# A hand-written order of 1,087 operations replaced by a new one, with four of six groups of filler matmuls left out

## The chip, the core and the metric

The kernel runs on one core of a Trainium2 chip. The metric is the device time of one execution in microseconds (us); lower is better. The engines named below are PE (TensorE, the matmuls), DVE (VectorE), ACT (ScalarE), POOL (GpSimd) and SP (SyncE, which issues nearly all DMAs).

## What is computed

The reference is a block with two residual halves on an input of 2048 rows and 640 columns, all in bf16, with scales and shifts made from a vector `c`:

```python
mod = (silu(c) @ w_mod)                     # sa, ca, ga, sb, cb, gb: 640 each
h = layernorm(A_q) * (1 + ca) + sa
k_shift = short_conv(A_k, shift_k)          # four taps along the rows
kv = k_shift * A_v
y = irfft(rfft(kv, 4096) * rfft(ssm_k, 4096))[:2048] + kv * ssm_D
x = A_q + ga * (h * y)                      # first half: long convolution
h = layernorm(x) * (1 + cb) + sb
z = gelu(h @ w_in)                          # 2 x 864 columns
z2 = layernorm(z[:, 864:])
g = w_sp @ z2 + b_sp                        # the mix: 2048 x 2048 over the rows
out = x + gb * ((z[:, :864] * g) @ w_out)
```

## The kernel before

**Convolution.** The 640 columns are cut into five units of 128. For each unit the filter (K) and the signal (U) go through the same steps. `stage1` multiplies the data by a table and leaves the tile `X1`. `forward` (line 432) makes eight blocks of frequencies in the PSUM tile `pu`. For K, `k_item` copies a block into a tile `KH` on ACT. For U, `u_item` multiplies `pu` by `KH` on DVE (the product of line 463, in `Tf` or `T`). In half of the blocks two sums on POOL or DVE follow (line 477, tile `W`). PE then multiplies back into `pz` (`inv`), and ACT or DVE copies the result into `Z`. The signal itself comes from `short_conv`: PE applies the four taps, DVE multiplies by v (line 570), and two DMA transposes of unit 0, or one of each other unit, regroup the result (line 582, tile `X`). For units 0 to 3 a DMA transpose turns `Z` into the single buffer `ZT` (line 708). PE makes y from it and DVE multiplies y into `gh` (line 701). Unit 4 is turned on PE instead (line 744). k and v of units 1 and 2, and of units 3 and 4, lie together in one buffer each (`kv_home`, line 512); this is the same in both kernels.

**First normalization and modulation.** `xt` is read in four DMAs of 640 KB (line 589). `ln1` takes statistics of each of 16 row tiles, on DVE (lines 603 and 604) or ACT (599 and 600). `mod` loads a slice of `w_mod` (line 643) and multiplies by `silu(c)`.

**Second half.** For each of four groups of four row tiles, `z_group` normalizes x, turns it (group 0 on PE, line 881; the others by a DMA transpose, line 912) and applies scale and shift (`hmod`, line 894, and `hmod2`, line 920). It then does 16 products with `w_in` of five matmuls of 432 columns. Each goes to a buffer `pu` or `pz`, and there are two of each. ACT applies gelu (line 943) and so frees the buffer. DVE takes statistics of the second half (line 949). POOL makes the reciprocal deviation `rstdz` (line 190), DVE makes `nmrz` (line 958), and `zn` on DVE (966) or ACT (964) normalizes.

**The mix.** The product with `w_sp` uses seven block products instead of eight, on sums made by DVE (lines 1011 and 1021). The seven products of the first pair of row tiles (`prodw`) stand in the ordered list. Pairs 1 to 7, with the projection by `w_out` (line 1160), follow as plain code.

**What sets the order.** Every operation up to and with the first pair is entered in a list (`Plan.op`) with the engines that may run it and what it depends on. `Plan.run` then issues the operations in the order of the string `ORDER`, on the engine that its letter names (P, A, D, G for POOL, S for SP):

```python
for e, i in order:
    o = self.ops[i]
    assert e in o["eng"] and done.issuperset(o["deps"]), (e, i)
    o["fn"](engines[e])
    done.add(i)
```

Each engine runs its own operations strictly in that order. An operation whose input or buffer is not ready holds up all that stand behind it on its engine, DMAs on SP included. A filler is a group of matmuls of the identity whose result nobody reads. They have no effect on the output:

```python
for j in range(k):
    mm(p_[:, 0:2], ident[:], ident[:, None, :].to_broadcast([P, S1C, P]), j == 0, j == k - 1)
```

Before, six groups of 4, 6, 2, 2, 4 and 3 of them stand in the list, as operations 1033 to 1038.

Of the kernel before, what the change touches and what calls it, by code (L numbers as in the profile page):

```python
# [30 lines left out]
PE_FLIPS = (4,)  # L31
TB = 4
NQ = DU // 4
FILLS = (4, 6, 2, 2, 4, 3, )
MODE = ('susussus', 'susussus', 'susussus', 'susussus', 'susussus')
SLOTS = dict(Tf=2, W=2, X=4, X1=4, KH=7, T=2, Z=3, ZT=1, wm=1, big=2, dg=2, st1=2, s1=1, sm=2, pu=2, pz=2)
PSUM_TAGS = ("s1", "sm", "pu", "pz")


ORDER = """  # L40
D0 P1034 A1 P7 D18 D128 D13 D15 A4 S89 D14 A16 D101 S2 G5 D6 P8 G102 D103 D116 D117 A10 A11 P1038 A28 A129 S90 D91 D17
P1035 A118 A119 S23 P146 P149 D104 S25 D105 A106 A107 D27 P1036 A147 P29 A148 P31 G108 S24 A150 G109 S26 D92 P155 D110
D111 A112 D151 A113 A156 G120 G121 P152 A154 A153 G114 D30 D32 G115 D20 P33 D122 D123 A124 A157 A125 G126 S524 D34 P35
D36 S525 D528 D529 D530 P1033 P158 A159 P162 A163 P134 P164 A135 A165 P166 A167 P137 D19 A21 P140 D141 P168 G127 S93
A169 P170 S37 S38 A171 D138 P172 A173 D94 P228 A229 D22 P174 A176 G139 P177 A179 D531 D175 D178 P234 S39 D235 G136 G41
P180 A181 D182 D532 P183 P230 A184 G53 A185 P186 D187 G142 A231 P202 D203 G42 P43 A533 D130 P232 G188 D189 S40 D44 P45
D46 S52 P196 D197 A534 G198 G199 S527 P160 A161 P190 A191 A233 P49 D50 P47 G54 D48 P212 P204 P248 S3 A535 P200 A205 P9
A249 P143 D213 G214 G215 D543 A12 G67 G131 G132 P222 A144 G145 D223 P55 D56 P192 D193 D536 G537 P59 D60 A544 A545 S51
P57 P252 A253 D58 P206 D207 G208 G209 P194 A201 S566 P218 D219 D538 G550 G551 P254 A195 A255 S526 D539 D540 P567 A568
S95 P569 A570 P258 A259 P216 P236 A237 P242 A243 G224 G225 P256 D257 P238 A217 A239 A541 P61 D62 S571 D96 S65 P210 S64  # L50
G66 P240 A241 P260 P220 D261 A211 G554 A546 P302 A303 P292 G555 G556 G557 A221 P574 G262 G263 D542 G552 D293 D547 P246
A247 P226 A227 S63 P572 P286 D287 D288 D553 P304 A305 D573 P264 A265 P250 A251 G78 P294 A295 P308 A309 D575 D652 G548
D549 G562 D592 P296 D297 G289 P276 A558 G298 P68 P306 S576 D277 P72 D615 P244 P290 A133 D559 A307 P270 D271 P326 A245
D69 P278 A291 G563 G564 P316 D73 A327 A565 D598 A317 P266 P328 A329 A279 D267 G299 P300 D301 P577 P314 S97 A315 P330
A331 G272 G273 D594 P324 A325 G613 D650 D578 S77 D593 D614 P70 D71 A560 A561 G617 P310 A311 P332 A333 G595 D714 D671
P280 D281 P74 D98 P579 D596 D75 P322 A323 P274 P350 A79 D351 G282 P376 A377 G283 P344 D345 D580 G654 A275 P268 A269
P334 D335 P378 G599 A379 P80 D597 P312 S600 A313 D81 P284 G346 G347 P320 P601 D602 A285 A321 P380 G336 G337 D708 G709
P366 A381 P370 D367 D371 P82 P382 A383 P318 G619 A319 P603 P338 P348 A349 A339 D83 S76 P388 A389 P400 D604 P605 D606
A401 S99 D100 P360 D361 P352 A353 P386 A387 P402 D620 G618 G372 G373 A403 P607 D608 P374 D375 P398 A399 G362 P354 G363
D355 G610 D356 G357 D616 P404 G653 A405 P364 P86 P384 A365 G656 P406 A407 D87 A385 P340 D341 P84 P368 D85 P408 P414  # L60
D409 A369 P450 P342 A451 P390 S621 P622 D415 G710 A391 G711 G677 D623 G410 G411 P454 A455 P418 P396 D419 A343 P624
P358 S581 P452 A397 D625 A453 G651 G420 D421 P392 P440 A393 P626 D627 P412 D441 G657 P456 A359 P428 G678 A413 G655
A457 D429 G430 G431 P628 D629 G630 P416 A417 P394 A395 P422 D423 S88 P474 A475 P464 A465 D635 P444 D445 G446 P582 A583
P480 A481 D636 P424 D425 P442 A443 D675 G676 D637 P458 A459 G447 P476 A477 D638 P434 D435 P426 D427 P472 A473 S658
P659 D660 P478 A479 P432 P466 P661 A433 P482 P448 A467 D609 D632 A449 D662 P663 G436 G437 P438 A439 P462 A463 D483
P498 D664 P665 D499 G673 G484 G485 P518 P486 D519 P502 D503 D504 P500 A501 G674 P460 A461 P468 A469 D666 P488 D489
A487 S584 G672 P585 A586 P508 G520 G521 P522 G505 A523 G668 D509 P492 D493 P506 A507 P470 A471 S679 P680 D681 P514
D515 G510 P490 A491 G511 G494 G495 P512 G715 G667 D634 A513 P682 D683 P516 A517 D631 P684 D685 P496 S757 D639 D633
P686 D687 D688 D690 A497 P720 A721 P716 G693 P722 P718 D717 P724 D719 P726 A723 P727 D689 P725 D728 G698 D729 D730
D759 D731 D760 G761 D696 D732 D733 D692 D762 G763 D735 A764 S587 P588 A589 P736 P1037 P590 A591 D734 D691 D772 D773  # L70
G774 P750 P765 D737 D738 D767 D769 D768 P766 A771 A770 D775 P743 D741 D837 G712 D697 P792 D751 S758 A777 P815 A816
D694 G776 P779 A783 A784 D742 P785 D739 D835 A786 D695 D740 P778 D836 D838 D752 A793 D713 D744 D745 G703 G839 D840
G841 G842 D843 P788 D782 A789 D781 D780 G612 D794 P795 A796 P817 P819 D670 D797 D669 D702 D700 D706 D611 G640 D642
A844 S845 D749 A818 P799 A800 G847 D641 D644 A820 D747 D902 P821 G846 D705 D701 D801 D645 D699 A822 P823 A824 D643
D904 P802 A803 D804 P806 A807 P825 A826 D805 A848 P813 A850 P827 A828 P809 A810 D849 A814 P851 A852 D746 P875 A876
D901 P879 A880 P858 A859 D748 D903 D790 D787 D811 P872 A873 D808 G905 D906 P865 S1046 P889 A866 A890 D648 P881 D704
A882 D756 D646 D812 D753 D967 D907 D909 G908 D754 D1050 P861 A862 D1047 P854 A855 D867 P893 A894 S1042 P883 A884 D798
G910 S911 P887 A888 A916 P891 A892 D877 P868 A869 D647 D968 P885 A886 D755 D969 D649 D707 D970 D1051 G971 D972 S1040
D791 S1039 A973 D976 D914 D975 D974 D853 D1052 G912 S1045 G913 G915 D856 P959 A960 P917 A918 D857 G829 D830 S977 G982
D874 D878 P947 A948 D834 D831 D860 D832 D833 D1063 D870 P920 A921 P924 A925 P938 A939 S1044 D863 D864 P931 S1041 D1055  # L80
D1056 P941 A942 D1058 D926 D979 G980 P927 A928 A932 G978 D1048 P953 D919 D933 D871 D929 P934 D940 P949 A954 D922 A981
P1000 D1054 P997 D923 S1043 A935 D936 G895 D896 D899 D1059 A950 P983 D930 A998 D999 D1060 A1001 D1002 A984 D943 D944
A898 A900 P993 A994 P1007 A1008 D937 D1057 G961 D897 D1064 D962 P1004 D985 D963 P990 P986 A987 D988 D989 A991 D992
D995 D996 A1005 D1006 P951 D1003 A952 A964 D965 P1025 P1015 A1016 D1009 D1010 A1026 D966 D1067 G1027 D1028 P955 A956
P945 A946 P957 D1030 P1021 A1029 P1013 D1032 A1022 A1014 P1071 P1073 A958 D1031 D1068 P1082 D1065 D1066 P1078 D1069
D1070 A1072 P1075 D1079 A1074 D1083 P1077 D1076 D1080 P1084 P1011 A1012 D1085 P1017 A1018 P1019 A1020 S1081 D1062
S1086 D1049 P1023 A1024 D1053 D1061
"""


# [39 lines left out]
def kernel(  # L130
# [79 lines left out]
    with ExitStack() as pctx:  # L210
# [758 lines left out]
        for g in range(NT // TB):  # L969
            z_group(g)  # L970
        for i, k in enumerate(FILLS):
            def fill(e, i=i, k=k):
                p_ = new("fill%d" % i, "s1", [P, S1C, 2 * NJ * 4], F32)
                for j in range(k):
                    mm(p_[:, 0:2], ident[:], ident[:, None, :].to_broadcast([P, S1C, P]), j == 0, j == k - 1)
# [258 lines left out]
```

## Time and profile before

| | |
|---|---|
| time, median of 3 runs | 312.26 us (312.03 to 312.69) |
| the profiled execution, its own time | 312.08 us |
| its span, first to last instruction | 310.0 us |
| PE busy | 296.2 us, 96% |
| DVE busy | 259.6 us, 84% |
| ACT busy | 157.0 us, 51% |
| POOL busy | 123.0 us, 40% |
| DMA moved | 42.63 MB, mean 137 GB/s |

Times within the execution count from the start of the span. A row of the profile gives the source line, the engine, the operation as output <- input, and how often it occurs. After a bar, or in brackets, stands the idle time of the engine before it and what ended it. "Busy" of PE is modelled, since matmuls overlap; how far apart they start tells more. Convolution and modulation fill the first 132 us. The products with `w_in` and the first pair of the mix go on to 205 us, and pairs 1 to 7 fill the rest.

### The profile page before, as it was taken

Reading aid. Unit: us, or ns where it says so; the run is one execution under the profiler, and the core shown is the slowest. Engines: PE = TensorE matmul, PEld = TensorE weight load, DVE = VectorE, ACT = ScalarE, POOL = GpSimd, SP = SyncE. Lnnn points to the kernel's source line nnn. Section 1 sums busy time; section 2 is a strip of 40 time slices with the busy share of each in tenths; the row PEclk is TensorE's granted clock in tenths of the full one; section 3 lists DMA queues with packets and bytes.
Section 4 is the critical chain, followed back from the end, with each engine's and each line's share of the span. In section 5 each row is a group of like instructions: output and inputs, shape, how many; then the busy total and the mean of one; then the engine's idle time right before and its main releaser. Section 6 shows DMA issues by size and latency. Waiting matters only on the chain.

```text
span 310.0 us, 6894 instructions
## 1 busy us (share of the span) xinstructions
PE 296.2 (96%) x2746; PEld 207.1 (67%) x2746; DVE 259.6 (84%) x528; ACT 157.0 (51%) x282; POOL 123.0 (40%) x157
## 2 busy tenths in 40 slices
PE   6989999999999998999999997999999999999996
PEld 2779898889999887755554553555565656555564
DVE  7999899999899999999969998957676858567474
ACT  5899899897969755476665684040101010010100
POOL 2663788859899696676342522000000000000000
PEclk9999999999999999999999999999999999999999
DMA  7999989986396779204999900092939395640614
GB/s 147 275 176 250 244 220 252 225 169 132 26 231 134 173 134 323 76 3 85 216 175 147 183 2 2 0 140 63 194 89 187 63 176 111 129 102 0 104 30 114
DMA packets 122963, 42.63 MB, mean 137 GB/s; under 512 B 108751, under 2 KB 122932, under 8 KB 122932
## 3 DMA queue, kind: packets, MB, share of 16 engines
q1 hardware_dynamic: 122778, 42.16, 64.6%
q8 instruction: 21, 0.34, 0.4%
q14 instruction: 10, 0.08, 0.1%
q10 hardware_dynamic: 154, 0.05, 0.1%
HBM read 16.11 MB, written 2.62 MB: 60 GB/s over the span
## 4 chain that ended last, share of the span: by engine, by line
PE 63%; DVE 25%; DMA 4%; issue 3%; ACT 2%; POOL 2%; POOLq 1%; DVEq 0%; ACTq 0%
PE ps L1036 23%; PE pu L244 12%; PE po L1160 10%; PE pz L244 8%; PE sm L244 4%; DVE st L949 3%; DVE Tf L463 3%; DMA ZT<-Z 3%; PE s L244 2%; PE pz L1036 2%; DMA KH<-in_c_dram 2%; DVE T L463 2%; DVE X L570 2%; DVE gh L684 1%; DVE st L603 1%
## 5 line engine op out<-in xcount | busy, mean ns | idle before, releaser
L244 PEld LDWEIGHTS <-Z 128*128 128x128 bf16 x320 | 30.9, 98 | 28.2 <-POOL Z L920 1.5
L244 PE MATMUL pu<-X,M 128*128 128x128 bf16 (+1 forms) x480 | 45.7, 237 | 1.9 <-ACT X L247 0.7
L244 PEld LDWEIGHTS <-M 128*128 128x128 bf16 x480 | 37.3, 98 | 6.3 <-issue 3.1
L1036 PEld LDWEIGHTS <-S 128*128 128x128 bf16 x256 | 25.0, 98 | 24.0 <-issue 2.4
L1042 ACT COPY m<-ps 128x432 f32<-128x432 f32 x7 | 3.6, 519 | 72.7 <-PE ps L1036 72.7
L477 POOL TENSOR_TENSOR W<-Tf 128x256 bf16<-128x256 f32 x45 | 33.2, 759 | 10.2 <-DVE Tf L463 8.3
L247 ACT CAST X<-s 128x1024 bf16<-128x1024 f32 x30 | 30.6, 1021 | 4.9 <-PE s L244 4.5
L1160 PE MATMUL po<-w_o,uT 128*128 128x320 bf16 (+2 forms) x231 | 32.7, 295 | 0.0
L244 PE MATMUL pz<-big,Z 128*128 128x432 bf16 x160 | 32.4, 346 | 0.3 <-POOL Z L920 0.3
L244 PE MATMUL pu<-big,Z 128*128 128x432 bf16 x160 | 32.3, 346 | 0.3 <-DVE Z L894 0.3
L463 DVE TENSOR_TENSOR Tf<-pu,KH 128x1024 f32<-128x1024 f32 x25 | 30.2, 1216 | 2.0 <-PE pu L244 1.7
L1036 PEld LDWEIGHTS <-wT 128*128 128x128 bf16 x192 | 18.7, 98 | 15.2
L1160 PEld LDWEIGHTS <-uT 128*128 128x128 bf16 (+1 forms) x231 | 22.2, 98 | 9.7
L244 PEld LDWEIGHTS <-G 128*128 128x128 bf16 x330 | 24.8, 98 | 1.7 <-issue 0.2
L247 ACT CAST Z<-pz 128x512 bf16<-128x512 f32 x36 | 20.9, 596 | 7.7 <-PE pz L244 7.5
L247 ACT CAST KH<-pu 128x512 bf16<-128x512 f32 x40 | 23.4, 595 | 2.1 <-PE pu L244 1.8
L1036 PE MATMUL ps<-X,wT 128*128 128x432 bf16 x112 | 22.7, 346 | 0.0
L1036 PE MATMUL ps<-T,S 128*128 128x432 bf16 x112 | 22.7, 346 | 0.0
L1036 PE MATMUL ps<-X,S 128*128 128x432 bf16 x112 | 21.6, 346 | 0.0
L244 PEld LDWEIGHTS <-X 128*128 128x128 bf16 x288 | 17.9, 97 | 4.8 <-issue 1.6
L244 PE MATMUL sm<-dg,big 128*128 128x128 bf16 x320 | 20.5, 219 | 0.2 <-DVE gca_bf L671 0.2
L244 PEld LDWEIGHTS <-big 128*128 128x128 bf16 x320 | 18.8, 98 | 0.6 <-issue 0.3
(189 smaller groups left out, 563.5 us busy)
## 6 DMA issues: line engine op xcount, KB each, us to landing
wm<-in_w_mod_dram SPq DMA_DIRECT2D x6, 800.0 KB, 5.6
xt<-in_A_q_dram SPq DMA_DIRECT2D x4, 640.0 KB, 7.3
out_dram<-ot SPq DMA_DIRECT2D x15, 160.0 KB, 2.0
big<-in_B_w_in_dram SPq DMA_DIRECT2D x2, 1080.0 KB, 5.9
X<-in_A_ssm_k_dram SPq DMA_DIRECT2D x4, 512.0 KB, 7.0
big<-in_A_v_dram SPq DMA_DIRECT2D x2, 1024.0 KB, 6.3
w_o<-in_B_w_out_dram SPq DMA_DIRECT2D x6, 160.0 KB, 3.0
X<-in_A_ssm_k_dram SPq DMA_DIRECT2D x2, 256.0 KB, 3.8
```

The costliest lines, as they stand in the source:

```text
L244: nc.tensor.matmul(o, lhsT=w, rhs=x, start=start, stop=stop)
L247: (e.copy if e is nc.scalar else e.tensor_copy)(dst, src)
L463: e.tensor_tensor(T_[:], (tl[pu] if src is None else tl[src])[:, :, :, None, :].to_broadcast(shape), tl[KH][:, :, None, :, :].to_broadcast ...
L477: e.tensor_tensor(tl[W][:, :, o, :], T_[:, :, 0, o, :], T_[:, :, 1, 1 - o, :], op=ALU.add if o else ALU.subtract)
L570: e.tensor_tensor(tl[kv][:].rearrange("p c (n g) -> p n c g", g=8)[:, 4 * i:4 * i + 4], tl[ps][:].rearrange("p a (c g) -> p a c g", g=8), ...
L603: e.bn_stats(out=st[:, a, :], in_=xt[:, n, a * HS:(a + 1) * HS])
L684: lambda e, vec=vec, o=o: e.tensor_tensor(gvu, gvu, vec[:, None, d0:d0 + du].to_broadcast([P, TB, du]), op=o),
L949: op("D", "stz", lambda e, i=i, n=n, fc=fc: e.bn_stats(out=stz[:, n, fc, :], in_=tl[z2][:, i, fc * FC:(fc + 1) * FC]), r=[(z2, (i, fc))], ...
L1036: nc.tensor.matmul(ps[:, :FC], lhsT=lhs[:, s_, :], rhs=rhs(s_), start=(s_ == 0 and not more), stop=(s_ == HT - 1), skip_group_check=more)
L1042: nc.scalar.copy(part[p, m][:], part[p, BANK[m]][:, :FC])
L1160: nc.tensor.matmul(ps[:, :hi - lo], lhsT=uTs[t][:fsz[ft], ft, :], rhs=w_o[:fsz[ft], ft, lo:hi], start=(ft == 0), stop=(ft == NFT - 1))
```

## The change

Two things differ in the file: the tuple `FILLS` and the string `ORDER`. No function is changed. Operations up to 1032 keep their numbers; the later ones fall by four, because four fillers are gone (`prodw` 1071 is now 1067).

```diff
-FILLS = (4, 6, 2, 2, 4, 3, )
+FILLS = (4, 6)
...
-D0 P1034 A1 P7 D18 D128 D13 D15 A4 S89 D14 A16 D101 S2 G5 D6 P8 G102 D103 D116 D117 A10 A11 P1038 A28 A129 S90 D91 D17
-P1035 A118 A119 S23 P146 P149 D104 S25 D105 A106 A107 D27 P1036 A147 P29 A148 P31 G108 S24 A150 G109 S26 D92 P155 D110
...
-P945 A946 P957 D1030 P1021 A1029 P1013 D1032 A1022 A1014 P1071 P1073 A958 D1031 D1068 P1082 D1065 D1066 P1078 D1069
-D1070 A1072 P1075 D1079 A1074 D1083 P1077 D1076 D1080 P1084 P1011 A1012 D1085 P1017 A1018 P1019 A1020 S1081 D1062
-S1086 D1049 P1023 A1024 D1053 D1061
+A4 A1 S89 D101 G5 D0 D18 P1033 G102 D103 D110 P7 S2 D13 D6 S90 D19 A21 P8 D111 A11 A112 D14 A10 D20 D22 D15 S23 D27
+S26 P1034 A16 D17 D91 P146 A28 A113 G114 A147 D92 P152 D104 D105 A107 A106 D148 A154 A153 D116 D117 P155 D157 G108
...
+D992 D996 D1043 D1006 D1010 P1021 D962 D965 A963 P957 A960 A1016 P1013 A1022 D964 A958 D966 D1063 P1067 P1025 G1027 D1028
+A1029 A1014 A1032 A1026 P955 D1060 P1069 D1061 D1030 D1031 D1062 A1070 D1064 A956 D1065 D1066 A1068 S1038 P1074 D1075
+P1078 S1037 D1079 P1071 D1055 P1073 D1072 D1076 P1080 D1081 S1077 P1011 A1012 P1019 A1020 P1017 A1018 P1023 A1024
+D1057 S1082 D1049 D1044 D1056 D1058
```

Per engine, the new list makes these changes. Eleven filler matmuls are gone; ten remain, four at the start and six right after the small transposes. Some operations change engine:

| operation (line) | DVE | ACT | POOL |
|---|---|---|---|
| sums of a product (477) | 5 -> 11 | | 45 -> 39 |
| copy of the back-transform table (247, `G`) | 2 -> 4 | 2 -> 0 | |
| first normalization `xn` (629, 631, 633) | 2 -> 4 | 4 -> 4 | 10 -> 8 |
| `stage1` copies (247, `X`) | 6 -> 5 | 42 -> 43 | |
| copies into `Z` (247) | 4 -> 3 | 36 -> 37 | |
| copies of unit 4's turned `Z` (247, `X`) | 2 -> 1 | 2 -> 3 | |
| residual sum (721) | 12 -> 10 | | 9 -> 11 |
| normalization of z2, `zn` (964, 966) | 12 -> 9 | 4 -> 7 | |
| second normalization `zx` (866, 868, 870) | 6 -> 6 | 4 -> 5 | 6 -> 5 |
| `hmod2` (918, 920) | 3 -> 2 | 4 -> 5 | 8 -> 8 |

SP issues the same 59 operations of the list in another order. Up to the second quarter of `xt` and its neighbours:

```
before: ... v0 v0' xt0 xt1 ldX1 | regroup0 regroup0' | k1 v12 k2 xt3 c ...
after:  ... v0' v0 k0' ldX1 xt0 k1 | regroup0 regroup0' | xt1 v12 xt3 k2 c ...
```

The first half of `w_in` (1080 KB, line 846) stood after the fourth transpose of `Z` into `ZT`. It now stands between the regrouping of unit 4 and the third transpose of `Z`. In the second half the order of SP changes too:

```
before: turn1 w_out w_sp turn2 w_sp w_sp bias turn3 w_sp w_sp w_sp
after:  turn1 w_sp w_sp w_out turn2 w_sp turn3 bias w_sp w_sp w_sp
```

More of the change, by code (lines that the diff above doesn't have):

```diff
@@ L40 @@
 ORDER = """
-D0 P1034 A1 P7 D18 D128 D13 D15 A4 S89 D14 A16 D101 S2 G5 D6 P8 G102 D103 D116 D117 A10 A11 P1038 A28 A129 S90 D91 D17
-P1035 A118 A119 S23 P146 P149 D104 S25 D105 A106 A107 D27 P1036 A147 P29 A148 P31 G108 S24 A150 G109 S26 D92 P155 D110
-D111 A112 D151 A113 A156 G120 G121 P152 A154 A153 G114 D30 D32 G115 D20 P33 D122 D123 A124 A157 A125 G126 S524 D34 P35
-D36 S525 D528 D529 D530 P1033 P158 A159 P162 A163 P134 P164 A135 A165 P166 A167 P137 D19 A21 P140 D141 P168 G127 S93
-A169 P170 S37 S38 A171 D138 P172 A173 D94 P228 A229 D22 P174 A176 G139 P177 A179 D531 D175 D178 P234 S39 D235 G136 G41
@@ L46 @@
[L46 to L84, printed above, removed]
-P945 A946 P957 D1030 P1021 A1029 P1013 D1032 A1022 A1014 P1071 P1073 A958 D1031 D1068 P1082 D1065 D1066 P1078 D1069
@@ L86 @@
-D1070 A1072 P1075 D1079 A1074 D1083 P1077 D1076 D1080 P1084 P1011 A1012 D1085 P1017 A1018 P1019 A1020 S1081 D1062
-S1086 D1049 P1023 A1024 D1053 D1061
+A4 A1 S89 D101 G5 D0 D18 P1033 G102 D103 D110 P7 S2 D13 D6 S90 D19 A21 P8 D111 A11 A112 D14 A10 D20 D22 D15 S23 D27
+S26 P1034 A16 D17 D91 P146 A28 A113 G114 A147 D92 P152 D104 D105 A107 A106 D148 A154 A153 D116 D117 P155 D157 G108
+A156 A115 P29 S25 D30 P149 A150 A151 D122 G109 D123 A125 A119 S24 P33 D34 A124 A118 G120 G121 S93 D94 S524 D128 G126
@@ new lines @@
+P35 A129 G42 P162 D36 S39 G127 P31 D32 P228 S37 S38 D528 A163 A229 P158 A159 S525 P137 P164 A165 D529 D530 D138 P234
+P166 A235 S40 P168 P134 A167 D135 P230 A169 A231 G54 P172 A173 P174 D531 D175 G136 A176 P232 D53 D130 P140 S527 A233
+P180 D181 A182 P170 A171 P183 D185 A184 P177 P45 A179 A178 P186 D532 G139 A533 A534 A535 P202 D141 D187 D203 G41 P43
+D44 D46 G188 P196 P212 A543 G189 D197 P190 P204 G198 G199 A205 A191 D213 G214 G215 P47 D48 P49 D50 P160 A161 G142 D536
+G537 P192 D193 S52 P55 D56 P200 S3 P206 D207 G208 G209 P57 D58 A544 A545 P248 A249 P194 P143 D144 G145 P242 A201 S526
@@ new lines @@
+A195 D539 P218 D219 A243 P9 A12 G131 G132 D538 S51 P252 A253 G554 A546 P59 S566 D60 P222 P216 S95 D223 P254 A255 P236
+A237 A217 P567 A568 P569 P258 A259 S571 P246 A247 G555 P210 D540 D541 D542 P238 A239 G224 G225 D211 P226 P256 A257
+A570 P61 P240 A241 S65 D96 P302 D547 A227 G550 D62 P260 D261 D262 A303 P220 P286 D287 G556 P574 D575 G263 A221 P304
+A305 A67 G548 S64 P292 D293 G78 P264 P572 D573 G288 G289 D549 D558 S63 P250 A251 D66 P308 A309 S576 A562 A563 P296
+D297 P294 A551 P270 G559 G560 D271 G272 P306 P276 D277 A295 P70 P68 P266 D265 P244 A307 D267 D69 D71 A564 D565 D598
@@ new lines @@
+A245 P278 A279 P326 G561 P290 G654 D298 D299 A327 P316 A317 D596 P310 A311 G273 P274 S77 G552 D553 P328 A329 P314 P577
+P579 A315 P324 D675 D557 A325 D594 D578 D595 P330 A331 P322 A323 D708 D615 G616 D599 D580 A291 P72 S97 D73 P280 D281
+A275 G671 G282 G283 G655 S600 P332 A333 P74 P312 A313 P300 A301 D98 P376 G617 A377 D592 P344 D597 A79 P268 D75 A269
+D345 P350 D351 P378 A379 P284 G593 P334 D335 G336 D337 G346 P80 D81 P318 A319 S76 G619 P380 A381 P601 D602 P366 D367
+D347 G677 P320 G620 P338 A321 P382 A383 A285 P603 D604 P82 D83 P370 D371 G372 D373 A339 P388 A389 P348 P400 S99 A401
@@ new lines @@
+P605 D606 P352 P386 A387 P360 P402 A403 D672 D613 G614 P607 D100 D652 P384 A385 P84 S581 P404 A405 D361 D362 P340 G363
+A353 D608 D610 P398 P86 S621 P406 D341 D673 A399 G618 D87 D85 A349 P396 A407 A397 P354 D355 D712 P368 A369 P450 A451
+P408 D409 G674 P342 A343 P414 P454 A455 S88 P374 A375 D612 P622 G678 D415 P364 A365 G656 D623 P392 A393 G356 D357 P452
+A453 G410 P624 D625 P390 A391 P358 G657 P418 S757 A359 D650 P626 P456 P582 A457 D627 P628 P440 G411 P412 A413 A583
+D419 G653 D441 P474 A475 G420 G421 P428 D429 G710 G430 G431 P416 P444 A417 G714 P480 A481 G651 P424 D445 D425 P442
@@ new lines @@
+D443 P394 A395 P476 A477 P434 P464 P432 A465 P478 A479 S658 P422 D435 P458 A459 G446 G436 D447 D437 D629 P659 D660
+A433 P482 A423 P472 G609 P661 P448 A449 D483 G484 A473 P438 G645 A439 D662 P498 D499 P426 A427 P663 D664 P466 A467
+G640 G485 P518 D519 G520 S584 G630 P665 P462 D635 A463 P585 G521 P460 P502 P486 A461 A487 D666 D503 P488 D489 P500
+A501 G504 P468 A469 G505 P522 A523 D632 P508 P506 D633 D509 A586 P492 D493 A507 S679 P490 A491 P470 G676 A471 P680
+P514 D510 G511 P512 A513 D681 D515 G494 P682 G495 P496 D637 D683 G668 D636 A497 S587 P516 A517 D634 P684 D685 P716
@@ new lines @@
+P686 A717 D638 P720 D631 D687 D688 G709 A721 S758 G667 P718 D719 G693 D690 D689 P722 D696 P724 P725 A723 D694 P726
+P727 D728 D729 D731 D730 D759 G711 D760 G761 D692 P736 D732 D733 D735 P588 P750 D734 D762 A763 G764 D691 D737 D773
+D772 G774 D738 P590 D741 A589 A591 P765 D767 D769 D768 P766 A770 P743 G611 A771 D775 A777 P795 A776 P785 A786 D837
+D739 D835 G715 D697 G703 D639 D742 D838 P817 P778 D695 D740 D836 G839 D751 D752 A796 A818 P779 A783 P819 A820 D713
+D744 D840 G841 D844 G669 A842 D782 A784 D780 D843 D781 P815 A816 D745 D747 D749 A133 P788 P792 A793 D646 S845 D748
@@ new lines @@
+D755 D698 D699 D746 G670 S1035 S1036 S1042 D702 D707 D641 A789 D701 D901 P825 A826 D642 D644 P827 A828 P809 A810 P823
+G850 A824 P799 A800 A847 P813 A814 G848 D647 A849 D904 P806 A807 P802 A803 D704 P821 A822 D846 P858 P851 A859 D643
+D903 D797 P893 A894 P889 A890 P887 A888 A852 P854 A855 P881 A882 P868 A869 P891 A892 D649 P872 P883 A873 D756 D700
+D970 A884 P865 A866 D902 G905 D705 D753 D906 G907 D908 P875 A876 D794 D798 D967 D909 D804 D706 G910 S911 A913 D860
+D1051 D1052 D1048 D801 P879 G915 A880 P885 G916 G912 D870 A886 P861 D1053 S1039 D811 D808 D812 D856 D805 D648 A862
@@ new lines @@
+D754 D968 D853 D857 D969 G971 D914 P934 P917 D1045 D1046 D972 G973 D975 D867 D976 A974 S977 P938 D877 A935 A918 D863
+D864 P924 A925 A939 D790 P927 D787 D791 S1041 G829 A928 G978 D1054 D874 D929 D940 D936 P920 A921 P941 A942 P953 A954
+D919 D871 A979 G980 P931 G981 D878 G895 D943 D922 D923 D926 D930 A932 D933 D937 D1050 D830 D833 D944 P951 A952 A982
+D832 D896 D898 S1040 P947 A948 G961 P949 A950 A834 D831 P983 A984 D1059 P986 P1000 A987 A900 P990 A991 A1001 P997 D988
+D985 D1047 D989 D1002 A998 D999 D1003 P1007 A1008 D1009 P993 A994 A897 P945 P1004 A946 A1005 P959 P1015 A899 D995 D992
@@ L88 @@
+D996 D1043 D1006 D1010 P1021 D962 D965 A963 P957 A960 A1016 P1013 A1022 D964 A958 D966 D1063 P1067 P1025 G1027 D1028
+A1029 A1014 A1032 A1026 P955 D1060 P1069 D1061 D1030 D1031 D1062 A1070 D1064 A956 D1065 D1066 A1068 S1038 P1074 D1075
+P1078 S1037 D1079 P1071 D1055 P1073 D1072 D1076 P1080 D1081 S1077 P1011 A1012 P1019 A1020 P1017 A1018 P1023 A1024
+D1057 S1082 D1049 D1044 D1056 D1058
 """
```

## Prediction

> **What bounds the kernel now.** I read the page's busy line first, then the stages, then the waits, then single stretches of the timeline and SP's own rows.
>
> ```profile
> PE 296.2 (96%) x2746; PEld 207.1 (67%) x2746; DVE 259.6 (84%) x528; ACT 157.0 (51%) x282; POOL 123.0 (40%) x157
> ...
> 0.00:27.00 27.00, 22.86 (x247) 17.45 (x248) 25.09 (x76) 21.86 (x47) 12.53 (x28) 1.00 1.00 211
> 27.00:60.00 33.00, 31.73 (x421) 28.99 (x420) 30.61 (x55) 30.70 (x59) 25.28 (x34) 1.00 1.02 239
> 60.00:100.00 40.00, 39.69 (x563) 36.93 (x561) 38.07 (x54) 34.50 (x53) 34.11 (x37) 1.00 0.69 137
> 100.00:132.00 32.00, 29.53 (x520) 26.20 (x516) 30.39 (x57) 18.40 (x33) 24.36 (x30) 1.00 0.68 176
> 132.00:205.00 73.00, 70.24 (x393) 37.17 (x390) 67.57 (x172) 43.02 (x79) 26.75 (x31) 1.00 0.51 92
> 205.00:310.00 105.00, 102.17 (x624) 60.32 (x621) 67.88 (x120) 8.51 (x15) 0.00 (x0) 1.00 0.52 107
> ```
>
> The columns of a stage are its length, then busy time of PE, weight loads, DVE, ACT and POOL, then granted clock, DMA share and GB/s. PE and DVE are both above 92% in every stage up to 205 us. Behind that, pairs 1 to 7 run on PE without a hole and are not touched. So only 0 to 205 us can move.
>
> Busy PE overstates PE. The timeline spaces five matmuls of 432 columns by 0.91 us and sixteen of 128 columns by 0.89 us, so a matmul takes 2.5 ns plus 0.417 ns a column. Counted so, PE has 285.3 us of work in the span. Between starts it loses 20.0 us more than that work, all before 193 us: 5.5 up to 30 us, 2.2 up to 60, 1.0 up to 100, 7.9 up to 140 and 3.3 after. The 5.5 and the 7.9 are where DVE decides: it is hardly ever idle there, and PE waits for its products, copies and `hmod`. From 60 to 100 us the two run level.
>
> **The change part by part.**
>
> *Fillers.* Eleven go; at 512 columns each is 0.216 us, in all 2.4 us of PE. Seven stood before 14 us, where PE waits for DVE and DMA. Four stood at 127.7 us, where PE waits for normalized rows (the first `w_in` matmuls stall until 132.6 for `hmod`, line 894). The waits that they filled become idle time, so I take 0. If PE has no slack after all, the first seven give back 1.5 us. For a loss there is one reason:
>
> ```profile
> 1.64 2.74 PE L244 MATMUL s<-ident 128*128 128x512 bf16 x6 [1.64 <-DVE ident L288]
> ...
> 127.72 1.02 PE L244 MATMUL s<-ident 128*128 128x512 bf16 x4
> ```
>
> Less the length of the last one (0.60 and 0.38 us), the first group is spaced by 0.43 us and the later one by 0.21: PE starts at half clock. The Trainium skill ("TensorE: Matmul & The Clock Gate", "What's actually happening") says that about 3.4 us of activity release the clock and one such idle window takes it away again. By that rule a thinner start (four fillers, a gap, six) may be slow for one window more. That doubles the first eight `stage1` matmuls, +0.9 us on DVE's first copies. The trace has no longer idle stretch of PE than 2.2 us (at 190) and the granted clock stays 1.00 over it, so I expect no later throttling. I take 0 and keep -1.5 and +0.9 as ends.
>
> *Work moved between engines.* Before the first `hmod`, DVE gets six sums more at 0.34 us start to start (+2.1), two table copies (+1.2) and two `xn` (+1.2) at 0.6, and one residual sum and one statistic (+0.7). It loses `stage1` copies (-1.8), one copy into `Z` (-0.6), one of unit 4's (-0.6) and joined small steps of `ln1f` (-1.4). Sum: +0.8 us on the busiest engine. POOL sheds 6.5 us there. DVE rows stretch beside a busy POOL (the two `turns` take 0.62 us together at 5.2 us and 0.96 at 11.4), about 6 us over this stage by my count of medians, so some 0.4 comes back. I take +0.4 (0 to +0.8). After that point DVE has 3.1 us less (three `zn`, three residual sums, one `hmod2`, one statistic), which matters only at the end of the stage. ACT's extra 7 us lie in its idle time there.
>
> *The second quarter of `xt`.* Every step on SP counts, as SP is strictly in order:
>
> ```profile
> 14.69 3.53 SPq L582 DMA_TRANSPOSE X<-X  x2
> 18.26 2.35 SPq L532 DMA_TRANSPOSE big<-in_A_k_dram  x1
> ...
> 26.88 0.58 SPq L589 DMA_DIRECT2D xt<-in_A_q_dram  x1
> ```
>
> Before, this quarter was issued at 8.4 us. Now it stands behind unit 0's two regroupings, and those wait for DVE's last product of unit 0. That product now stands about 1.4 us later in DVE's order (steps of the signal's table 0.65, one `stage1` copy more 0.6, an add 0.2). So they run from 16.1 to 19.6 us. The load lands 5.2 to 7.3 us after its issue: the earliest is behind the second regrouping's landing (4.7 us after its issue) plus 2.7 us for 640 KB at the 239 GB/s of this stage; the latest is the 7.3 of a quarter issued at 33.9. That is 24.8 to 26.9 us. DVE reaches its first statistic of that quarter (line 603) at 23.5 before, and at about 23.6 now. It waits 1.2 to 3.3 us, and behind it stand the first two products of unit 0, for which PE waits. Some of it is covered, as PE and ACT can still finish filter blocks. I take +1.5 (0 to +3.3).
>
> *The first half of `w_in` ahead of the third `ZT`.* `ZT` is a single buffer, so its transpose starts after the last y of the unit before:
>
> ```profile
> 89.16 4.33 SPq L582 DMA_TRANSPOSE X<-X  x1
> ...
> 96.96 4.82 SPq L708 DMA_TRANSPOSE ZT<-Z  x1
> ...
> 105.38 0.41 PE L244 MATMUL sm<-Ebd,ZT 128*128 128x64 bf16 x8 [0.36 <-DMA ZT<-Z]
> ```
>
> It lands in 8.4 us. Between those two points the old order has 7.6 us of PE work, so PE waited 0.4. The new one has 8.4, so this wait goes: -0.4. But 1080 KB now enter the rings a few microseconds before. The regrouping at 89.16, issued right after an 800 KB load, landed in 7.9 us where the same one at 70.2 took 4.3. I expect the load to be issued at 89 to 92 us and to land 5.9 later, and the transpose at 94.7. The overlap is 0.8 to 3.3 us, and there is no slack left. As the first descriptors alone are hit, I take +0.5 (0 to +3.6).
>
> *Two waits near 33 us* (0.76 of PE for `c`, 0.72 of DVE for `xt`) go, since both loads move ahead of the 5.5 us transposing load. They lie at one place: -0.7 (0 to -0.9).
>
> *Between 132 and 205 us.*
>
> ```profile
> 188.71 1.62 PE L1036 MATMUL pu<-X,wT 128*128 128x432 bf16 x8
> 192.48 1.62 PE L1036 MATMUL pz<-T,S 128*128 128x432 bf16 x8 [2.15 <-ACT G L943]
> ...
> 190.65 0.16 DVE L958 SCALAR_TENSOR_TENSOR nmrz<-mvz,rstdz 128x4 f32<-128x4 f32 x1 [0.90 <-POOL rstdz L190]
> ...
> 190.91 1.11 ACT L964 ACTIVATE X<-X,nmrz,rstdz 128x864 bf16<-128x864 bf16 x1 [4.20 <-DVE nmrz L958]
> 191.92 0.93 ACT L943 ACTIVATE G<-pz 128x432 bf16<-128x432 f32 x2
> ```
>
> ACT stands 4.2 us at a `zn` that waits for the last `nmrz`. The gelu behind it holds the buffer `pz` that the second product needs. In the new order 47.0 us of DVE work lie between the first `hmod` and that `nmrz`, before 51.9; PE's second product stands at 57.3 us of PE work in both. Following the rows through: the last aggregate at 51.5 us after `hmod`, `nmrz` at 54.0, two `zn` of 1.1 and two gelus to 57.7, the product at 58.0. So the 2.15 us go, with 0.3 to spare: -2.2. If a `zn` is late by more than that, each us comes back one for one.
>
> The 0.6 us at 163 us for group 2's turned rows should shrink. DVE reaches that group's `nmr2` 2.5 us earlier in its own work, although three loads (9.4 us) instead of two (6.3) stand ahead of the turn on SP: -0.5 (-0.6 to +1). Loads of `w_sp` and `w_out` now land only just before DVE's `ssum` and `gbm` near 152 us. That may idle DVE 1 to 2 us, hidden as long as DVE's `hmod2` of group 2 comes over 4 us before PE needs it.
>
> *The sum*, against the profiled execution's own 312.08 us (2.08 around the span; the median of the runs is 0.18 above it): -2.2 - 0.5 - 0.4 - 0.7 + 0.4 + 1.5 + 0.5 + 0 = -1.4, so **310.7 us**. The smallest difference that a measurement of this kernel can tell from none is about 0.2%, 0.6 us.
>
> **The rivals.**
>
> *PE was the bound.* If waits of PE for DVE shrink once fillers and the waits at 33 us are gone, the seven fillers pay 1.5 us and the `ZT` overlap is hidden (0 for 0.5): -3.4, 308.7 us. For it: 60 to 100 us at full PE. Against: DVE has 0.8 more to do before `hmod`. Chance 0.20.
>
> *The load of `w_in` holds up the third `ZT`* by the 3.6 us of the row at 89.16 instead of 0.5: +1.7, 313.8 us, slower. The place is the y of unit 2 near 103 us; it decides from a landing 2.5 us later than the 8.4 (the 0.5 counted and 2.0 more). Against: the load is about to land when the transpose starts. Chance 0.20.
>
> *The wait at the end stays.* ACT has three more `zn` there, 1.1 us each, before the gelus that free `pz`. If the 2.15 us remain, +0.8: 312.9 us. Chance 0.15.
>
> The new order does take the fillers out and does move the loads, so doing nothing is no rival.
>
> **How the numbers follow.** The likeliest case (0.45) is 310.7, its own range 309.0 to 312.3; I give 0.37 of it to faster, 0.06 to the same and 0.02 to slower. The second case (0.20) is all faster. The `w_in` case (0.20) is 0.01 same, 0.19 slower. The last (0.15) is 0.07 same, 0.08 slower. Together faster 0.57, same 0.14, slower 0.29. The range, 307.5 to 314.3, takes in all four values and, below, the seven fillers with the `xt` wait hidden.
>
> **What would show it.** Right: no wait of a `pz` product for gelu near 190 us; a DVE row of line 603 waiting for `xt` near 24 us; the first `w_in` matmul within 1 us of 132.6; PE at granted clock 1.00 after 5 us. Wrong: line 603 without a wait; a `ZT` wait above 1 us near 103; a new idle stretch of ACT at line 964 with PE behind it; or the first `w_in` matmul moved by more than 3 us, which would mean that the order as a whole, and not these places, decides.

## The result, and the profile after

The changed kernel takes 309.59 us (median of 8 runs, 308.57 to 311.30), the kernel before 312.30 us (8 runs beside them). The ratio is 0.9918, with a 95% interval of 0.9896 to 0.9940. It is faster by 2.7 us, where 1.6 was forecast. The profiled execution took 309.58 us, 2.50 us less than that of before. Its span is 307.81 us (310.04 before), 2.24 us less; the other 0.27 us lie outside the span.

First the busy line of the page and the stages of the changed kernel, with the columns of the prediction's first fence:

```profile
PE 294.5 (96%) x2735; PEld 206.6 (67%) x2735; DVE 256.9 (83%) x528; ACT 162.5 (53%) x293; POOL 116.3 (38%) x146
...
0.00:27.00 27.00, 22.54 (x237) 16.91 (x238) 24.29 (x77) 22.37 (x49) 11.18 (x25) 1.00 1.00 210
...
100.00:132.00 32.00, 28.78 (x496) 25.93 (x495) 30.48 (x58) 19.78 (x33) 25.64 (x30) 1.00 0.54 139
132.00:205.00 73.00, 72.41 (x415) 38.87 (x412) 65.36 (x165) 49.58 (x89) 25.64 (x32) 1.00 0.49 96
```

Only one stage has changed its character. From 132 to 205 us PE goes from 70.24 to 72.41 us busy, DVE from 67.57 to 65.36, and ACT from 43.02 to 49.58. In the four stages ahead of it, taken together, busy PE is 1.7 us lower (eleven fillers at 0.216 us are 2.4) and busy DVE 0.7 us higher.

The end of that stage, in the timeline of the changed kernel:

```profile
186.37 0.15 DVE L958 SCALAR_TENSOR_TENSOR nmrz<-mvz,rstdz 128x4 f32<-128x4 f32 x1
...
186.80 1.12 ACT L964 ACTIVATE X<-X,nmrz,rstdz 128x864 bf16<-128x864 bf16 x1
186.95 1.62 PE L1036 MATMUL pu<-X,wT 128*128 128x432 bf16 x8
...
190.24 1.62 PE L1036 MATMUL pz<-T,S 128*128 128x432 bf16 x8
```

The last `nmrz` comes 4.28 us earlier than the 190.65 of before, none of these rows shows idle time ahead of it, and the second product of pair 0 starts at 190.24 instead of 192.48. That is 2.24 us. The first three `hmod` on DVE, in the kernel before and then in the changed one:

```profile
131.52 1.04 DVE L894 TENSOR_SCALAR Z<-s,cb_col,sb_col 128x256 bf16<-128x256 bf16 x3
```

```profile
131.48 1.03 DVE L894 TENSOR_SCALAR Z<-s,cb_col,sb_col 128x256 bf16<-128x256 bf16 x3
```

The third of them (operation 768) starts at 132.11 us (132.16 before). This is the moment called "the first `hmod`" from here on, and the place at which experiments split the list. So in this pair of traces the whole gain lies behind it. I started from that: **the end of the list pays (theory A)**. The rivals were that the fillers were PE's own time (B), and that the new order of the front pays (C).

### The profile page after: what moved, and what is told of

Its sections match the earlier page's. It is cut to its first block, busy times and chain, and to the rows that moved or that the text cites. A ratio compares the mean times of both kernels' runs of the same rounds, so it can differ in the third digit from the quotient of the medians.

```text
span 307.8 us, 6885 instructions
## 1 busy us (share of the span) xinstructions
PE 294.5 (96%) x2735; PEld 206.6 (67%) x2735; DVE 256.9 (83%) x528; ACT 162.5 (53%) x293; POOL 116.3 (38%) x146
## 4 chain that ended last, share of the span: by engine, by line
PE 76%; DVE 12%; ACT 6%; issue 2%; DMA 2%; POOL 0%; DVEq 0%; POOLq 0%
PE ps L1036 23%; PE pu L244 17%; PE pz L244 14%; PE po L1160 10%; PE sm L244 4%; PE s L244 3%; DVE Tf L463 3%; DMA X<-X 2%; PE pz L1036 2%; ACT KH L247 2%; ACT X L247 2%; DVE st L727 2%; PE pu L1036 1%; DVE T L463 1%; DVE gh L701 1%
## 5 line engine op out<-in xcount | busy, mean ns | idle before, releaser
L477 POOL TENSOR_TENSOR W<-Tf 128x256 bf16<-128x256 f32 x39 | 29.6, 775 | 19.0 <-DVE Tf L463 16.9
L247 ACT CAST X<-s 128x1024 bf16<-128x1024 f32 x32 | 32.9, 1027 | 4.2 <-PE s L244 4.2
L949 DVE BATCH_NORM_STATS2 st<-X 128x6 f32<-128x432 bf16 x32 | 18.0, 590 | 3.2 <-ACT X L943 3.0
```

Of the source, the lines that this page charges most:

```text
L247: (e.copy if e is nc.scalar else e.tensor_copy)(dst, src)
L477: e.tensor_tensor(tl[W][:, :, o, :], T_[:, :, 0, o, :], T_[:, :, 1, 1 - o, :], op=ALU.add if o else ALU.subtract)
L949: op("D", "stz", lambda e, i=i, n=n, fc=fc: e.bn_stats(out=stz[:, n, fc, :], in_=tl[z2][:, i, fc * FC:(fc + 1) * FC]), r=[(z2, (i, fc))], ...
```

## The experiments

In rows of the experiments the source lines are lower by one than in the kernels before and after, except in the repetition of the changed kernel. Each run is set against runs of the kernel before on the same chip. Operations keep their numbers of before up to 1032.

### Fillers out of before, fillers into after

```diff
 (before)
-FILLS = (4, 6, 2, 2, 4, 3, )
+FILLS = (6, 4, )
...
 (after: 3 ahead of P146, 2 ahead of P29, 2 ahead of P33, 4 ahead of P765)
-FILLS = (4, 6)
+FILLS = (4, 6, 3, 2, 2, 4, )
```

> The kernel before with the four groups of fillers taken out that the change takes out (11 matmuls), the order otherwise as before. Theory A (the gain comes from the end of the list, between the first hmod and the mix): the waits that the fillers covered become idle time, 312.3 us, +-0.4, and the clock is granted in full about a microsecond later or not at all later. Rival B (the fillers were PE's time): 312.3 - 11 x 0.216 = 309.9 us.

> The changed kernel with 11 fillers put back: 3 ahead of the first stage1 matmul, 2 and 2 among the early ones, 4 ahead of the first transposes of the mlp half (op 765). Theory A: 309.6 us, +-0.4. Rival B: 309.6 + 2.4 = 312.0 us.

Measured: 312.06 us against 312.51, ratio 0.9973 (0.9943 to 1.0002), and 310.02 us against 312.51, ratio 0.9920 (0.9894 to 0.9945). Neither moves by 2.4 us, so B is out. By the medians, taking the fillers out of before gains 0.45 us, and putting them into the changed kernel costs 0.2 to 0.8 us (it stands 2.7 and 3.3 us below before in its two measurements, this one 2.5). These runs hardly tell that from nothing.

The first trace shows that this is not because nothing happened. Stretches of before without its fillers, with granted clock in the third column from the end:

```profile
127.00:136.00 9.00, 8.02 (x134) 5.95 (x131) 8.28 (x31) 3.38 (x6) 6.02 (x9) 0.62 0.01 3
136.00:200.00 64.00, 63.35 (x355) 34.14 (x354) 60.07 (x153) 39.85 (x74) 23.43 (x28) 1.00 0.52 99
```

The clock fell to half at 129.05 us, right behind the place of the four fillers, and stayed there for 6.83 us. At the start it was granted in full only at 13.0 us instead of 4.55. The first `hmod` was 1.3 us later (133.41 us), and PE was 2.4 us later at the `w_in` product that begins at 136.66 before (139.04). Yet the second product of pair 0 started at 192.41 us, as before (192.48): it waits for the same gelu, and PE's loss went into that wait. I come back to the clock below.

### One half of the list old, one half new

```diff
 (run e3: old front, new end)
 before's ORDER up to and with D768, then what is left in after's order;
+D712 D612 G645 G640 S758 D694 D741   <- done by the new front, so now first behind D768
...
 (run e4: new front, old end)
 after's ORDER up to and with D768, then what is left in before's order
+A133 G715 D639 G698 stay behind D768
```

> The order of before, its fillers included, up to and with the first hmod (op 768); from there what is left in the order of after. Theory A (the end pays): 312.3 - 2.2 = 310.1 us. Rival C (the front's new order pays): 312.3 us or above, since the front is the old one.

> The order of after, its two groups of fillers included, up to and with the first hmod (op 768); from there what is left in the order of before. Theory A: 312.3 us, the wait of a pz product for its gelu near 190 us is there again with about 2 us. Rival C (the front's new order pays): 310.1 us or below. Where C and A both hold in part, the gains of this run and of the run with the old front add up to 2.7 us.

Measured: 311.64 us against 312.51, ratio 0.9969 (0.9949 to 0.9989), for the new end; 309.86 us, ratio 0.9913 (0.9889 to 0.9937), for the new front. That is the opposite of theory A: the new front (with the fillers left out there) brought the whole gain and the new end a third of it. Had I stopped here, I would have written that the front pays. The traces say otherwise. First the run with the new end:

```profile
135.69 1.73 ACT L865 ACTIVATE Z<-xt,nmr,rstd 128x640 bf16<-128x640 bf16 x2 [2.98 <-DVE nmr L855]
...
137.48 0.51 PE L880 MATMUL s<-ident,Z 128*128 128x128 bf16 x6 [1.86 <-ACT Z L865]
```

PE loses 2.0 us (start to start) to rows that ACT normalizes late, because `nmr` is late on DVE. Ahead of it on DVE stand D712, D612, D694 and D741, in all 2.6 us. The first two are POOL's work in before. The hybrid has made its own wait. At the end of the list the waits of before are gone: no row of line 1035 there waits.

Now the run with the new front:

```profile
188.70 0.16 DVE L957 SCALAR_TENSOR_TENSOR nmrz<-mvz,rstdz 128x4 f32<-128x4 f32 x1 [0.90 <-POOL rstdz L189]
...
190.53 1.62 PE L1035 MATMUL pz<-T,S 128*128 128x432 bf16 x8 [0.64 <-ACT G L942]
```

Here too the gain is made at the end: the first `hmod` is at 131.67 us (0.5 us early), the second product of pair 0 at 190.53 (1.95 us early). The wait for the gelu has shrunk from 2.15 to 0.64 us, since `nmrz` is 1.95 us earlier. The front reaches the end through DVE's list: statistics 694 and 741 and residual sum 645 stand ahead of the first `hmod` now, and DVE is 1.0 us early at 146 us. DVE loses this lead at 154 us, to a wait for a gelu. But the turn of group 2 has been issued at 152.66 instead of 153.55 us, so at 160 us DVE no longer waits 1.3 us for its landing and is 1.3 us early. Two more pieces make it 1.95: a wait of 0.4 us for `rstdz` at 165 us is gone, and one sum of line 1011 takes 0.69 us at 169 us where it took 1.15.

### The new end without its own wait

```diff
 (run e3, behind D768)
-D712 D612 G645 G640 S758 D694 D741 P766 ...
+G712 S758 P766 ...            D741 ahead of D837, D694 ahead of D835
+G612 ahead of G669, G640 ahead of G670, D645 ahead of D646
```

> As in the run with the old front and the new end, but the steps that the new front had already done (residual sums 612, 640, 645, products 712, statistics 694, 741) stand near the places and on the engines that they had before, not in a block right behind the first hmod. Theory G (the new end needs DVE free right behind the first hmod; the block cost PE the 2.0 us at 137.5): that wait is under 0.7 us, and the end alone brings the gain of the whole change or nearly: 312.3 - 2.0 to 2.5 = 309.8 to 310.3 us. Rival (the end alone is worth no more than the 0.9 us of the first such run): 311.4 us.

Measured: 310.44 us against 312.48, ratio 0.9936 (0.9912 to 0.9960). The same rows of PE start without a wait:

```profile
135.51 0.50 PE L880 MATMUL s<-ident,Z 128*128 128x128 bf16 x6
```

The second product of pair 0 starts at 190.46 us, again without a wait. So the end alone is worth 2.0 us, and it gets there with all 21 fillers in. The front alone, its fillers left out, is worth 2.6 (e4), and both together 2.7 or 3.3. They do not add up, because they cut the same thing: the time from the first `hmod` to the last `nmrz`, and PE's wait behind it. Once it is gone, PE's own work sets the time.

### The wait by itself: one step moved in before

```diff
 (e5)
-P1021 A1029 P1013 D1032 A1022 A1014
+P1021 P1013 D1032 A1022 A1014 A1029
...
 (e6)
+D645 ahead of D794 (6 us earlier on DVE)
...
 (e7: both)
```

> The kernel before with one step moved: ACT's normalization of the last row block (zn 1029, line 964), which waits 4.2 us for the last nmrz, stands behind the gelus 1022 and 1014 instead of ahead of them. Theory D (the wait of 2.15 us at 190 us is ACT's order: a gelu that frees pz stands behind a waiting zn): the second product of pair 0 starts at about 190.3 instead of 192.5 us, 312.3 - 2.0 = 310.3 us. Theory E (it is the whole DVE list that ends too late, and the next product meets another row that is not there): 312.3 us, -0.5 at most.

> The kernel before with one other step moved: the residual sum 645 (DVE, line 721), for whose end at 146.2 us the load of w_out waits on SP for 3.2 us, stands 6 us earlier in DVE's order, ahead of the first statistic of z (stz 794). Theory F (the end of before is late because that wait on SP makes the turn of group 2 land late, DVE waits 1.3 us for it at 160.4, and with it everything up to the last nmrz): the turn is issued at about 152.7 instead of 153.6 us, nmrz at about 189 instead of 190.65, 312.3 - 1.5 = 310.8 us. Rival (that wait is absorbed by later waits of DVE): 312.3 us.

> The kernel before with both steps moved: the residual sum 645 ahead of stz 794, and zn 1029 behind the gelus 1022 and 1014. Theories D and F: no more than the 2.15 us and the 0.6 us of PE's waits at 190 and 163 us can go, 312.3 - 2.3 to 2.7 = 309.6 to 310.0 us, the time of the changed kernel. If instead the whole reorder is needed: 311.3 us or more.

Measured against 312.24 us: 311.22 (ratio 0.9955, 0.9933 to 0.9976), 312.26 (1.0005, 0.9979 to 1.0032) and 311.09 (0.9945, 0.9919 to 0.9971).

The end of the first of these:

```profile
190.21 1.62 PE L1035 MATMUL pz<-T,S 128*128 128x432 bf16 x8
190.68 0.16 DVE L957 SCALAR_TENSOR_TENSOR nmrz<-mvz,rstdz 128x4 f32<-128x4 f32 x1 [0.90 <-POOL rstdz L189]
...
193.31 0.89 PE L1035 MATMUL pz<-X,S 128*128 128x432 bf16 x4 [0.75 <-DVE X L1020]
```

The 2.15 us at the second product are gone (190.21 instead of 192.48), as theory D says. But `nmrz` is as late as before, and 3 us further on PE waits for the sums that DVE makes behind it: 0.91, 0.24 and 0.22 us, counted from start to start. 1.0 of the 2.0 us expected remains. So ACT's order alone takes half of the gain, and the other half needs `nmrz` itself earlier.

A part of that half shows in the clock of the single runs. Of the 29 runs of before beside these, 11 had a mean granted clock of 0.995 and a median of 313.8 us; the other 18 had 1.000 and 312.0. Of the 12 runs with the moved step (e5) none was below 0.999. Against the runs of before at full clock alone the step is worth 0.8 us. The last section comes back to this.

The second edit does nothing, and both together (e7) gain no more than 0.13 us over the first alone. In e6 the load of `w_out` is issued at 143.84 instead of 146.26 us, as meant, but the turn of group 2 only at 153.91:

```profile
143.84 3.37 SPq L1096 DMA_DIRECT2D w_o<-in_B_w_out_dram  x7
147.27 2.94 SPq L996 DMA_TRANSPOSE wT<-in_B_w_sp_dram  x1
153.91 3.08 SPq L911 DMA_TRANSPOSE Z<-Z  x1
```

SP now stands idle from 150.2 to 153.9, since the turn waits for rows that POOL and DVE normalize until then. Theory F took the first wait on SP for the one that counts. It is the rows, and so again the lists of the computing engines.

### The two loads that I had priced, put back

```diff
 (e8, in after)
+S525 ahead of S37
 ... A159
-S525
...
 (e10, in after)
-S757
 ... S658 ... S679
+S757
```

> The changed kernel with the load of the second quarter of xt (S525) put back ahead of the two regroupings of unit 0 on SP. If the place behind the regroupings costs what I forecast (+1.5): 309.6 - 1.5 = 308.1 us. If it costs what the trace shows as DVE's wait for it (0.4): 309.2 us. If the front is held by DVE anyway, or the regroupings are now late in its place: 309.6 us.

> The changed kernel with the first half of w_in (S757) put back behind the fourth ZT on SP, as before. Were the overlap with the third ZT worth the 0.5 us that I counted: 309.6 - 0.5 = 309.1 us. By the wait that the trace of after shows at that ZT (0.27 us, less than the 0.52 of before): 309.6 us, +-0.2. If the load is now late for the first product with w_in: above 310 us.

Measured: 309.28 us against 312.24, ratio 0.9896 (0.9863 to 0.9930), and 308.41 against 312.48, ratio 0.9872 (0.9841 to 0.9903). Both look like gains on the changed kernel, the second by 1.2 us. But its trace has the 0.9 us that its span is shorter by already at 42 us, in front of the load that it moves, and keeps them through every point between 74 and 131 us to within 0.04 us. The first, too, is level with after at 28 us and gains its 0.8 us between 30 and 42. So I measured the changed kernel again.

### The changed kernel again

> The changed kernel once more, unaltered, to size what two measurements of one kernel differ by. The run with w_in put back came out 1.2 us below the changed kernel, but in its trace the whole 0.9 us of the profile lie between 25 and 40 us, 50 us ahead of the load that it moves. If that difference is chance (when the transposing loads of that stretch land): 308.4 to 309.0 us here, or a spread that holds both values. If the moved load is its cause: 309.6 us, +-0.2.

Measured: 309.21 us (308.38 to 310.26, 8 runs) against 312.49, ratio 0.9896 (0.9861 to 0.9931). The values of the run before it lie within its spread. SP's queue shows what differs, first in the changed kernel, then in its repetition:

```profile
15.86 3.23 SPq L582 DMA_TRANSPOSE X<-X  x2
19.13 0.58 SPq L589 DMA_DIRECT2D xt<-in_A_q_dram  x1
...
32.81 3.20 SPq L582 DMA_TRANSPOSE X<-X  x1
```

```profile
15.86 2.64 SPq L582 DMA_TRANSPOSE X<-X  x2
18.54 0.58 SPq L589 DMA_DIRECT2D xt<-in_A_q_dram  x1
...
32.45 1.81 SPq L582 DMA_TRANSPOSE X<-X  x1
```

The same transposing DMAs of the same program hold SP for 3.23 or 2.64 us, and for 3.20 or 1.81. With the second of them goes a wait of PE at 39 us, 0.9 us long (start to start) in one trace and 0.1 in the other; 1.2 us in all at 42 us. Over both measurements the changed kernel has 16 runs with a median of 309.5 us. Moving `S525` back is worth nothing that these runs show. With `S757` it is not so clear: all six of its runs lie between 308.39 and 308.68 us, and only 3 of the 16 of the changed kernel lie as low. That is hardly chance. But in the one trace the lead begins 50 us ahead of the moved load, so why these runs are faster stays open.

### No fillers at all

```diff
-FILLS = (4, 6)
+FILLS = ()
```

> The changed kernel without its last ten fillers: no activity of PE before the first turns at about 4.3 us. If fillers only fill waits: 309.6 us, +-0.3. If they are there for the clock: full clock is granted at 10 us or later instead of 7.0 (13.0 us was seen with a thinned start of before), the first stage1 matmuls run at half speed, and 0.5 to 1.5 us are lost: 310.1 to 311.1 us. If they are PE's time: 307.4 us.

Measured: 309.78 us against 312.48, ratio 0.9909 (0.9879 to 0.9939): the same as with ten. In its trace full clock is granted at 12.08 us (7.00 in after), and the clock is down to half again from 128.14 us for 6.83 us. PE's idle time between starts grows by 1.8 us while 2.2 us of filler go. The two cancel.

## Why the prediction was right, and where it was not

The side and the place were right. By its number the result, 309.59 us, lies between my likeliest case (310.7) and the rival that PE was the bound (308.7), a little nearer to the rival. The rival's mechanism is not what happened: it needed 1.5 us from seven fillers, and the medians show 0.2 to 0.8 us for all eleven (the interval of e1 alone would reach 1.8).

The sum was 1.1 us short on the profiled execution: -1.4 forecast, -2.50 measured. Three errors make this up. Up to the first `hmod` it came out 1.3 us better than forecast. Behind it, it came out 0.5 us worse (-2.7 forecast, -2.20 measured). And 0.27 us of the gain lie outside the span, which I had taken as fixed. That the first two partly cancel is luck.

**The wait for gelu at 190 us (-2.2): confirmed.** I had counted `nmrz` at 54.0 us behind the first `hmod` and the second product at 58.0. The trace has 54.26 and 58.13. The rival "the wait at the end stays" was wrong by that: no `zn` was late. What I had not separated are the two causes in it: ACT's order is worth 1.0 us by itself (e5), and DVE's list the rest.

**`hmod2` at 163 us (-0.5): gone, as forecast.** In its place PE has three small waits between 136 and 139 us, 1.1 us together from start to start, for `gh` from DVE (line 769) and for the gelu (line 943). They were not in the forecast:

```profile
136.19 2.18 PE L244 MATMUL pz<-big,Z 128*128 128x432 bf16 x10 [0.34 <-DVE gh L769]
138.59 1.07 PE L244 MATMUL pz<-big,Z 128*128 128x432 bf16 x5 [0.23 <-ACT M L943]
```

**The second quarter of `xt` (+1.5): the step that failed by most.** It was issued at 19.13 us, 0.5 us earlier than the 19.6 that I counted, and its landing was put too late. My bounds were 5.2 to 7.3 us from issue to landing, the lower one from a regrouping that lands in 4.7 us; here that regrouping landed in 3.2 us, and the quarter 5.03 us behind its own issue. DVE used it at 24.18 us:

```profile
24.18 0.89 DVE L603 BATCH_NORM_STATS2 st<-xt 128x6 f32<-128x320 bf16 x2 [0.40 <-DMA xt<-in_A_q_dram]
```

The wait is 0.40 us, and in the repetition, where the load is issued at 18.54, there is none: a sign that I had named for being wrong. With the load back in front of the regroupings (e8) this wait is gone, but PE waits at 20.4 us for the regrouped tile instead, and nothing came back. The term is 0 to 0.4 us.

**`w_in` ahead of the third `ZT` (+0.5, its wait -0.4): both too large.** The load was issued at 90.36 us as forecast and landed 6.3 us later, at 96.66. The transpose was issued at 96.54, not at 94.7, so the two overlap by 0.1 us (my own figures give 0.2 to 3.2 us, not the 0.8 to 3.3 that I wrote). PE lost 0.27 us there instead of 0.52, and the same 0.27 with the load put back (e10). So the term is nothing and the rival of 3.6 us did not come about; what a longer overlap would cost was not measured.

**Two waits near 33 us (-0.7): moved, not gone.** The wait for `c` is away, but PE waits 0.1 to 0.9 us at 39 us for the regrouped unit 1, depending on the run.

**Up to the first `hmod`** the terms summed to +1.3 us (0.4 + 1.5 + 0.5 - 0.4 - 0.7). The traces have -0.04 and, in the repetition, -1.0. With the terms put right (0.4 or 0 for `xt`, 0 for the overlap, -0.25 for the `ZT` wait, +0.1 or -0.7 near 33 us, DVE's +0.4 kept) the sum is +0.65 in the one and -0.55 in the other. That leaves 0.7 and 0.5 us that I can't assign to a term. DVE's +0.4 was not measured by itself; its busy time up to 132 us grew by 0.7 us, the upper end of my range.

**Fillers (0): the size was right, the reason only half.** I wrote that their waits become idle time, that full clock is there after 5 us and that I expected no later throttling. The waits did become idle time, but the clock did change, at both places. Two fences, the start of the changed kernel, and one stretch of it in the first trace and then in the repetition:

```profile
2.46 1.89 PE L244 MATMUL s<-ident 128*128 128x512 bf16 x4 [2.46 <-DVE ident L288]
...
4.54 2.67 PE L244 MATMUL s<-ident 128*128 128x512 bf16 x6
```

```profile
127.00:134.50 7.50, 6.44 (x113) 4.61 (x110) 7.26 (x28) 3.83 (x7) 5.15 (x8) 1.00 0.02 3
```

```profile
127.00:134.50 7.50, 7.12 (x85) 4.44 (x82) 7.20 (x29) 4.99 (x8) 6.07 (x8) 0.54 0.00 1
```

At the start all ten fillers are spaced at half clock, and full clock came at 7.00 us instead of 4.55; this cost 0.2 us on the first `stage1` matmul (7.20 for 7.00 us). At 127 us the repetition ran at 0.54 of full clock. PE was 1.2 us early when it began and 0.6 us early when it was over, so it cost 0.6 us; in before without its fillers PE went from 0.9 us late ahead of the dip to 2.4 us late behind it. The bounds that I kept for this, -1.5 and +0.9, hold both ends.

**A reading that was wrong.** I wrote that PE and DVE are both above 92% in every stage up to 205 us. PE is at 85% in the first (22.86 of 27 us). No term of the sum rests on it.

## What to carry to other kernels

Where an engine with a strict order waits for a late result, ask which work queued behind it is needed sooner: moving one normalization behind two gelus was worth 1.0 us of the 2.7, and only shortening the list that makes the result late brought the rest. Undo a reorder in halves with care, since a hybrid makes waits of its own: the new end looked worth 0.9 us and was worth 2.0 once six displaced steps stood about where they had been. Before a gain below half a per cent is given to an edit, look where in the trace it begins, and run the unchanged kernel once more: 0.9 us of one experiment began 50 us ahead of its edit.

## What the runs showed of the hardware

**The clock falls for whole windows.** The dips in the traces last 6.83 us (three kernels without fillers at 127 us) or 3.41 us (after with its fillers put back), one or two times the 3.4 us that the Trainium skill gives as window ("TensorE: Matmul & The Clock Gate", "What's actually happening"). A run's mean granted clock tells them apart: 0.989 for the long, 0.994 or 0.995 for the short.

The long dip belongs to the place at 127 us. Of 52 runs of the six kernels without fillers there, 17 show 0.989. Of 139 runs of kernels with the four fillers there, none is below 0.994. That long dips follow the missing fillers is shown; what triggers them is not. It was no idle window, as in the rule that the prediction used: in the 3.41 us ahead of the dip in the repetition PE was busy for 2.98 us by the profile, and its longest wait from start to start was 0.53 us. In the medians these dips hardly show (before without its fillers: 312.2 us with the long dip, 311.9 at full clock), since PE waits for DVE at this place anyway.

Fillers do not keep the short dip away. Without the four, 9 of the 52 runs show one; before, with all its fillers, shows one (0.995) in 30 of its 77 runs beside the experiments. The median of these 30 is 313.5 us, that of the other 47 is 312.1. Of the four kernels with the same fillers and another order at 190 us (e3, e5, e7, e9) one run in 44 shows a short dip, and none does of the 12 of e5, which moves one step of ACT at 190 us. With that step left alone (e6) it is 4 in 12. So the order at 190 us, where PE of before waits 2.15 us, decides over this dip too, and some 0.4 us of the gain against these medians come from it (312.47 us over all 77 runs, 312.06 at full clock). No such run of before was traced, so that the dip lies behind this wait is inferred.

**The same start gets its clock at different times.** With the 17 fillers that before has at the front, full clock was granted between 4.4 and 5.4 us in four executions and at 10.1 and 10.2 us in two (e7 and e9, whose edits lie 120 us or more further on). With the ten of the new front it came between 6.0 and 8.0 us in five executions. The page named above puts this moment at around 4 us of sustained matmuls, give or take half a microsecond ("What you observe"). Counted from PE's first matmul at 1.64 us, the kernels with the front of before needed 2.7 to 3.7 us in four executions and 8.5 and 8.6 in two; PE's work there has gaps of a few tenths of a microsecond. In e7 and e9 the steps were 1.0 us late at 31 us and only 0.2 us at 33: before waits 0.9 us there for the load of `c`, from start to start, and these two runs 0.1.

**A transposing DMA's hold on SP is not fixed.** In two executions of the changed kernel the same issues took 2.64 and 1.81 us or 3.23 and 3.20 us, and at 42 us PE was 1.2 us earlier in the one with the shorter holds.
